# A segment-recurrent attention and a gated feed-forward on one core: softmax products split anew, query pieces in another order, weights loaded in halves, four feed-forward units moved into the loop

## The chip, the cores and the metric

The kernel runs on one core of a Trainium2 chip. Its engines run side by side: TensorE (PE in the profile, with its weight loads as PEld), VectorE (DVE), ScalarE (ACT), GpSimd (POOL) and SyncE (SP), which issues the DMAs. The metric is the device time of one execution in microseconds (us), the median of several.

## The reference

The input x has 2048 rows of 512. The first part, A, normalizes x and walks over it in 64 segments of 32 rows. The eight rows of memory that a segment's attention leaves are the first eight of the next segment's 40 rows, so the segments form a chain:

```
mem = mem0
for s in range(64):
    h = concatenate([mem, xs])            # 8 + 32 rows, 512 wide
    q, k, v = h @ Wq, h @ Wk, h @ Wv      # 32 heads of 128
    scores = q k^T * 128**-0.5            # masked, 40 x 40 for each head
    o = softmax(scores) v @ Wo
    mem = o[:8]; outs.append(o[8:])
```

The second part, B, takes h = x + A, normalizes it, computes z = gelu(h_n @ w_in) (1792 wide), splits z into z1 and z2 of 896 each, normalizes z2 over its columns, mixes it over rows with a 2048 x 2048 matrix w_sp, adds b_sp, multiplies by z1, and multiplies by w_out (896 x 512). The output is h plus that.

## The kernel before, in words

Everything is issued through an emitter: each operation names the tokens that it reads and writes, and the emitter makes the semaphore waits from them. The order of the calls is the order on each engine. Nothing is reordered later, so the order written in the file is what counts.

The kernel has three stages.

The *prologue* loads the weights in the order Wq, Wk, Wv, Wo. `load_w` (L304 to L309) loads a quarter of one of the first three (8 heads, 1 MB) with one DMA and one token. It normalizes the first rows of x, transposes them (`xT`, L383) and computes q and k of the x rows of chunk 0 (16 segments) and half of chunk 1 before the loop starts (`qkx_mm`, L418, called by `start_x`; one call is a group of 16 matmuls: four heads of Wq for i below 8, four of Wk from 8 on).

The *loop* runs over the 64 segments (L1035 on). The rows of x of a segment do not depend on the memory, so products of them alone for later segments are cut into units that fill the places where TensorE would wait for other engines. One list of units, `gx`, gives one whole unit to each segment, just before the products of the probabilities with V. A second list, `gv`, gives single quarters of a unit ("atoms"). `vx_group` units make V rows, `qkx_group` and `qkr_group` make q and k columns. In the last segments units of part B take their place: `z2_group` and `z2_atoms` compute the z2 half of z for 128 rows in narrow tiles (32 columns of the array at a time), 448 wide.

Within a segment, TensorE goes through these steps, and this order is written out by hand:

1. `QK` (L500, L501): q and k of the segment's 40 rows for two halves of the heads, in pieces of four matmuls of 512 columns, one piece for each 128 of the 512 inputs (dc 0 to 3). The pieces of the first two dc need the first half of the new memory, `hT`, which ACT copies (L707), and the others the second. Then `QK_evac`: ACT copies the sums into a staging tile `Tst` (L537), DVE transposes it from there into QT or KT (L549). `mask_put` (L561, DVE) writes the mask into the scores' bank. `K1` and `K1_transpose` (L527, L534) do the fourth product, in two halves.
2. `S_half` (L571, L577): scores of one half of the heads, on top of the mask. `sm_exp` (L585) on ACT, `sm_sums` (L592) on TensorE, `sm_ln` and `sm_rcp` (L603, L607) on ACT give the reciprocal R of the softmax denominators.
3. `V_half` (L500, in between) and `V_evac` (L635 on ACT, L637 on DVE): V of the segment.
4. `sm_norm` (L611): E times R, 160 columns of each half, on POOL for half 0 and on DVE for half 1; `sm_normx` (L617, DVE), the 64 columns against the x keys that the unit above prepared.
5. the unit from `gx` or `zx`, then `PV_half` (L645, L651), the scaling copies `cT_evac` (L664 ACT, L666 DVE), and `Wo`, which ends in `part` and `mem_out` (L702, L707): the next segment's memory.

A small planner (L1004 to L1030) keeps the instruction stream of TensorE in step with a period of 256 instructions: `tile_mm` can use a weight tile that the piece before has loaded (`held`, L501) or load it again (L500). `plan` weighs where the period's boundary falls in the next segments, and where it asks for it `hold` lets up to eight pieces load again, which adds four instructions each. Its constants are WAITS = 15 and 2 per segment.

*Stage B* starts after the loop. `z2_row` and `z2_mm` (L1264) make z2 for rows 13 to 15; rows 0 to 12 come back from DRAM. Then, for each of twelve row blocks in turn, it mixes a block (`mix0`, L1303, five matmuls), computes two groups of z1 (`z1_some`, L1296, four matmuls of 512 columns each, evacuated by ACT at L1299 with the gelu), and brings the z2 of the next block through gelu (L1327), statistics (L1278, L1280, DVE), the power on POOL (L1282, L1284) and the scaling (L1289, DVE). The 28 z1 groups are counted off in pairs; the mixing of the second to fourth quarter of the columns and the output products (L1420) follow.

Of the kernel before, what the change touches and what calls it, by code (L numbers as in the profile page):

```python
# [169 lines left out]
def fast_path(nc, st, keep, A_x, A_mem0, A_Wq, A_Wk, A_Wv, A_Wo, A_seg_len, B_w_in, B_w_sp, B_b_sp, B_w_out, out):  # L170
# [15 lines left out]
    CK = 16  # L186
# [71 lines left out]
    z2p_d = nc.dram_tensor("z2p_d", [NP, 128, FH], BF, kind="Internal").ap()  # L258
    wT_d = nc.dram_tensor("wT_d", [S // 64, 128, RB, 64], BF, kind="Internal").ap()
# [50 lines left out]

    load_xe(0, 0)
    load_xe(1, 1)
    for hq in range(4):
        load_w(0, hq)
# [95 lines left out]
    def qkx_mm(ck, i, bank, only_hh=None, only_dc=None):  # L410
        mi, h0 = i // 8, 4 * (i % 8)
        ws = (w_q, w_k)[mi]
        for hh in range(4):
            h = h0 + hh
            for dc in range(DC):
                if only_hh is not None and (hh, dc) != (only_hh, only_dc):
# [3 lines left out]
                   reads=[("hTe", ck % 3), ("W", mi, h // 8)], writes=[PB(bank)])  # L420
# [162 lines left out]
    def sm_exp(b):  # L583
        bank = SBK[b]
        act(lambda e: e.activation(out=E_sb[:, b, :], in_=ps[:, bank, 0:224], func=ACT.Exp, scale=scale, bias=SHIFT),  # L585
            reads=[PB(bank)], writes=[("E", b), ("Ex", b)])

    def sm_sums(b):
        bank = SBK[b]
        for c in range(4):  # L590
# [3 lines left out]
               reads=[("E", b), "ones"], writes=[PB(bank)])  # L594
# [15 lines left out]
    def sm_norm(b, on):  # L610
        on(lambda e: e.tensor_tensor(out=E_sb[:, b, 0:160], in0=R_sb[:, b, :], in1=E_sb[:, b, 0:160], op=ALU.mult),  # L611
           reads=[("R", b), ("E", b)], writes=[("E", b)])
# [6 lines left out]
    def V_half(s, b, dcs=range(DC), held=None):  # L619
# [3 lines left out]
        for dc in dcs:  # L623
            for c in range(4):
# [3 lines left out]
                   reads=[("hTx", (s // 4) % 3), ("hTm", s, dc // 2), ("W", 2, 2 * b), ("W", 2, 2 * b + 1)], writes=[PB(bank)])  # L628
# [10 lines left out]
    def PV_half(s, b):  # L639
        xb = s % NVX  # L640
        for g in range(4):
            for c in range(4):
# [5 lines left out]
                    reads=[("V", b, g // 2), ("E", b)], writes=[PB(PVB[c])])  # L648
# [162 lines left out]
    def z2_group():  # L811
        rb, hf = zx.pop(0)
        z2_narrow(rb, hf, XB)
        return lambda: z2_out(rb, hf, XB, "dve")

    def z2_atoms():
        rb, hf = zx.pop(0)
        mms = [lambda dc=dc: z2_narrow(rb, hf, VXB, (dc,)) for dc in range(DC)]
        gv.add(VXB, mms, lambda: z2_out(rb, hf, VXB, "act"))

    Z0 = 42

    def pour():
        if s >= Z0 and not gv.atoms and zx and s + 2 < NSEG:
            z2_atoms()
# [26 lines left out]
    act(lambda e: e.preload_act_table_set("natural_log_exp_and_others"))  # L852
    for j in range(2):
        ln_inplace(j)
    late_consts()
    xT(0, 6)
    xe_copy(0, 6)
    for hq in range(4):
        load_w(1, hq)
# [17 lines left out]
    for i in range(16):  # L877
        start_x(0, i)
        if i == 1:
            xT(1, 7)  # L880
            xe_copy(1, 7)
        if i % 2 == 1 and i > 2:
            start_x(1, i // 2 - 1)
        if 7 <= i < 10:
            ln_apply(i - 3)
        if 6 <= i < 9:
            ln_stats(i - 2)
        if i == 10:
            xT(4, 6)
            ring_copy(0, 6)  # L890
        if i == 12:
            xT(5, 7)
            ring_copy(1, 7)
        if i == 14:
# [3 lines left out]
    start_x(1, 7)  # L898
    for hq in range(4):
        load_w(2, hq)  # L900
# [69 lines left out]
    for ck, i0 in ((1, 10), (2, 0), (3, 0)):  # L970
# [3 lines left out]
        if i0:  # L974
            qkx_group(ck, 10)
            qkx_group(ck, 11)
        for mi, b in ((0, 0), (0, 1), (1, 0), (1, 1))[3 if i0 else 0:]:
# [26 lines left out]
    FETCH, FETCH0, WAITS = 256, 191, 15  # L1004
# [9 lines left out]
    def plan(s, start, depth=4):  # L1014
        n = 588 + 24 * (s % 4 == 2) + 8 * (s >= 3 * CK)
        best = None
        for k in range(9):
            c = 10 * block_cost(start, 4 * k, n) + k
            if depth > 1:
                c += plan(s + 1, start + n + 4 * k + 2, depth - 1)[0]  # L1020
# [12 lines left out]
    zx = [(rb, hf) for rb in (0, 4, 1, 5, 2, 6, 3, 7, *range(8, NP)) for hf in range(2)]  # L1033
    qx_copy(0)
    for s in range(NSEG):  # L1035
# [15 lines left out]
        spare[0] = plan(s, pe_count[0] + WAITS + 2 * s)[1] if s else 0  # L1051
# [11 lines left out]
        QK(s, 1, 0, (2, 0, 1, 3), 2, 3, hold(2))  # L1063
# [61 lines left out]
        sm_norm(0, pool)  # L1125
        sm_normx(0)
        V_evac(1, (0,))
        V_evac(1, (1,), "act")
        sm_norm(1, dve)
        sm_normx(1)  # L1130
        if s == 0:
# [3 lines left out]
            start_x(1, 8)  # L1135
# [4 lines left out]
        full = full or s >= 3 * CK  # L1140
        late = [] if full else pour()
        if s >= 3 * CK:
# [1085 lines left out]
```

## Time and profile before

| | |
|---|---|
| median of 3 runs | 845.12 us (843.77 to 845.2) |
| profiled execution | 842.99 us |
| its span, first to last instruction | 841.3 us |
| instructions | 44,814 |
| TensorE busy | 827.7 us, 98% of the span |
| DVE, ACT, POOL busy | 524.0, 469.1, 127.4 us |
| DMA | 77.29 MB, mean 92 GB/s |

The profile's times are microseconds from the first instruction. A row of a timeline gives the start, the length, the engine, the line of the kernel, the operation, what it writes and reads, its shape, how many instructions it stands for, and in brackets the idle time of the engine before it with what ended that. TensorE's ends are modelled, because its matmuls are pipelined: the next row often starts a little before the end of the last. For the length of a step the differences between starts are the better measure.

### The profile page before, as it was taken

How to read it: one execution, taken by the hardware profiler on the slowest of the kernel's cores; microseconds unless marked ns; L12 is line 12 of the kernel's file. 1: busy time of each engine (PE TensorE's matmuls, PEld its weight loads, DVE VectorE, ACT ScalarE, POOL GpSimd, SP SyncE). 2: the span in 40 equal slices, each digit the busy share in tenths (PEclk: the TensorE clock that was granted, in tenths of full speed). 3: DMA queues.
4: the chain of work that ended last, by engine and by line, in shares of the span. 5: the costliest groups of instructions: out<-in, count | busy, mean ns of one | idle time of the engine just before them, and what ended most of it. 6: DMA issues, size and time to landing. Idle time of an engine off the chain costs nothing.

```text
span 841.3 us, 44814 instructions
## 1 busy us (share of the span) xinstructions
PE 827.7 (98%) x21935; PEld 427.5 (51%) x18845; DVE 524.0 (62%) x1320; ACT 469.1 (56%) x1251; POOL 127.4 (15%) x340
## 2 busy tenths in 40 slices
PE   6999999999999999999999999999999999999998
PEld 6754445555555554555555545455555544444443
DVE  3555667666666666676766676666666666554443
ACT  3456566766666666666666666666666676500000
POOL 5111111111111111111211111111111123200000
PEclk9999999999999999999999999999999999999999
DMA  9962222222222232121323232333323298033001
GB/s 319 379 220 55 78 61 64 71 58 68 56 54 49 59 48 66 38 68 48 82 42 88 54 71 54 84 77 87 85 69 81 74 276 286 1 113 109 30 14 40
DMA packets 111252, 77.29 MB, mean 92 GB/s; under 512 B 64840, under 2 KB 100688, under 8 KB 111056
## 3 DMA queue, kind: packets, MB, share of 16 engines
q1 hardware_dynamic: 111056, 74.36, 31.1%
q8 instruction: 162, 2.65, 1.3%
q14 instruction: 34, 0.28, 0.1%
HBM read 42.38 MB, written 21.59 MB: 76 GB/s over the span
## 4 chain that ended last, share of the span: by engine, by line
PE 97%; DMA 1%; SPq 1%; issue 0%; DVE 0%; ACT 0%
PE f_ps L500 45%; PE f_ps L501 13%; PE f_ps L1303 12%; PE f_ps L729 4%; PE f_ps L1296 3%; PE f_ps L1420 3%; PE f_ps L645 3%; PE f_ps L437 2%; PE f_ps L797 2%; PE f_ps L418 2%; PE f_ps L571 1%; DMA f_arena<-in_A_Wk_dram 1%; PE f_ps L592 1%; PE f_ps L443 1%; PE f_ps L702 1%; PE f_ps L651 1%
## 5 line engine op out<-in xcount | busy, mean ns | idle before, releaser
L500 PE MATMUL f_ps<-f_arena,f_hT 128*32 128x512 bf16 (+1 forms) x4832 | 356.2, 356 | 0.3
L500 PEld LDWEIGHTS f_ps<-f_arena,f_hT 128*32 128x32 bf16 x4832 | 119.8, 96 | 155.6 <-issue 63.5
L501 PE MATMUL f_ps<-f_arena,f_hT 128*32 128x512 bf16 (+1 forms) x2336 | 186.7, 334 | 0.0
L537 ACT ACTIVATE f_Tst<-f_ps 128x512 bf16<-128x512 f32 x228 | 129.4, 597 | 60.3 <-PE f_ps L500 60.3
L500 PE MATMUL f_ps<-f_arena,f_cT 128*32 128x256 bf16 x3844 | 129.1, 272 | 0.9 <-ACT f_cT L664 0.5
L500 PEld LDWEIGHTS f_ps<-f_arena,f_cT 128*32 128x32 bf16 x3844 | 94.4, 96 | 29.0 <-ACT f_cT L664 19.1
L1303 PE MATMUL f_ps<-f_arena 128*128 128x512 bf16 x448 | 100.9, 379 | 0.0
L549 DVE STREAM_TRANSPOSE f_QT<-f_Tst 128x256 uint32<-128x256 uint32 x128 | 57.1, 446 | 67.5 <-ACT f_Tst L537 67.5
L637 DVE CAST f_V_sb<-f_ps 128x512 bf16<-128x512 f32 (+1 forms) x128 | 71.0, 555 | 41.9 <-PE f_ps L500 41.9
L666 DVE TENSOR_SCALAR f_cT<-f_ps 128x320 bf16<-128x320 f32 x128 | 56.9, 486 | 27.8 <-PE f_ps L651 27.8
L1303 PEld LDWEIGHTS f_ps<-f_arena 128*128 128x128 bf16 x448 | 43.7, 98 | 52.6
L585 ACT ACTIVATE f_E_sb<-f_ps 128x224 bf16<-128x224 f32 x128 | 46.2, 361 | 36.4 <-PE f_ps L577 36.4
L695 DVE CAST f_part<-f_ps 128x256 bf16<-128x256 f32 x64 | 27.2, 425 | 61.9 <-PE f_ps L500 61.9
L556 POOL COPY f_QT<-f_arena 128x128 uint32<-128x128 uint32 x64 | 18.7, 292 | 298.4 <-PE f_ps L577 298.3
L664 ACT ACTIVATE f_cT<-f_ps 128x320 bf16<-128x320 f32 x128 | 49.0, 435 | 22.6 <-PE f_ps L651 22.6
L707 ACT ACTIVATE f_hT<-f_ps 128x16 bf16<-128x16 f32 x126 | 23.2, 184 | 53.6 <-PE f_ps L702 53.2
L1309 DVE TENSOR_TENSOR f_arena<-f_ps,f_arena 128x512 f32<-128x512 f32 x28 | 19.3, 690 | 52.9 <-PE f_ps L1303 52.9
L561 DVE CAST f_ps<-f_mask 128x224 f32<-128x224 bf16 x128 | 47.0, 367 | 0.0
L607 ACT ACTIVATE f_R_sb<-f_R_sb 128x160 f32<-128x160 f32 x128 | 43.1, 337 | 4.0
L527 ACT ACTIVATE f_Tst<-f_ps 128x256 bf16<-128x256 f32 x128 | 42.1, 381 | 3.7
L686 POOL COPY f_cTx<-f_cT 128x256 bf16<-128x256 bf16 x64 | 25.4, 396 | 121.0 <-DVE f_cT L666 121.0
L693 ACT ACTIVATE f_part<-f_ps 128x256 bf16<-128x256 f32 x64 | 24.6, 384 | 31.4 <-PE f_ps L500 31.4
(123 smaller groups left out, 1202.1 us busy)
## 6 DMA issues: line engine op xcount, KB each, us to landing
wT_d<-f_wst SPq DMA_DIRECT2D x64, 128.0 KB, 2.3
f_arena<-wT_d SPq DMA_DIRECT2D x32, 256.0 KB, 4.9
f_arena<-in_A_Wq_dram SPq DMA_DIRECT2D x4, 1024.0 KB, 8.7
f_arena<-in_A_Wk_dram SPq DMA_DIRECT2D x4, 1024.0 KB, 14.0
f_arena<-in_A_Wv_dram SPq DMA_DIRECT2D x4, 1024.0 KB, 14.6
f_arena<-in_A_Wo_dram SPq DMA_DIRECT2D x8, 512.0 KB, 9.6
f_Vx<-vext_d SPq DMA_DIRECT2D x63, 64.0 KB, 2.7
vext_d<-f_Vs SPq DMA_DIRECT2D x24, 128.0 KB, 2.0
```

What stands on the lines that cost most here:

```text
L500: return e.matmul(out, lhsT=lhsT, rhs=rhs, start=start, stop=stop, skip_group_check=True, tile_position=(0, 32 * c))
L501: return e.add_instruction(mybir.InstMatmult(name=nc.get_next_instruction_name(), ins=[e.lower_ap(rhs), e.lower_ap(lhsT)], outs=[e.lower_a ...
L527: act(lambda e: e.activation(out=Tst[:, 1, 256 * k:256 * k + 256].rearrange("p (gi r) -> p gi r", r=2), in_=ps[:, bank, 0:256].rearrange(" ...
L537: act(lambda e: e.activation(out=Tst[:, tb, :].rearrange("p (C gi r) -> p C gi r", C=2, r=2), in_=ps[:, bank, :].rearrange("p (C r gi) -> ...
L549: dve(lambda e: e.transpose(out=dst, in_=Tst[:, mi, :].bitcast(U32)), reads=[("T", mi, 0), ("T", mi, 1)], writes=wr)
L561: dve(lambda e: e.tensor_copy(out=ps[:, bank, 0:224], in_=mask[:, :]), reads=["mask"], writes=[PB(bank)])
L585: act(lambda e: e.activation(out=E_sb[:, b, :], in_=ps[:, bank, 0:224], func=ACT.Exp, scale=scale, bias=SHIFT), reads=[PB(bank)], writes=[ ...
L607: act(lambda e: e.activation(out=R_sb[:, b, :], in_=R_sb[:, b, :], func=ACT.Exp, scale=-1.0, bias=RBIAS), reads=[("R", b)], writes=[("R", b)])
L637: dve(lambda e: e.tensor_copy(out=V_sb[:, b, cs], in_=ps[:, bank, cs]), reads=[PB(bank)], writes=wr)
L664: act(lambda e: e.activation(out=dst, in_=src, func=ACT.Copy, scale=UNSC), reads=[PB(PVB[c])], writes=[("cT", c)])
L666: dve(lambda e: e.tensor_scalar(out=dst, in0=src, scalar1=UNSC, scalar2=None, op0=ALU.mult), reads=[PB(PVB[c])], writes=[("cT", c)])
L1303: pe(lambda e: e.matmul(ps[:, bank, 0:TB], lhsT=z2[:, sc, fb * 128:(fb + 1) * 128], rhs=wTb[tb % 2][:, :, sc, :], start=(n == 0), stop=(n ...
```

## The change

Six things are changed together.

- *Prologue.* The first quarter of Wq is loaded by two DMAs. Wk and Wv are loaded in halves (2 MB, one DMA for both quarters' tokens). 40 and 12 matmuls on a constant tile are put ahead of the first transposition and after it. The groups of chunk 0 and chunk 1 are interleaved in pairs: all 16 groups of Wq first, then those of Wk; 28 groups stand before the loop instead of 24, and the units that are left for the loop begin at group 14 instead of 10. The four units of `qkr_group` for chunk 1 are no longer needed.
- *Query order.* The dc 0 piece of the product for half 1 of q moves ahead of the pieces that need the first half of the memory.
- *Softmax products.* The E token is split in two parts (columns 0 to 119 and 120 to 159). For half 1 DVE multiplies the first part and POOL the second, V's first half is evacuated ahead of `sm_normx(0)`, and PV's groups wait for the part of E that they read. The wait for Vx is moved to the last piece of `V_half`.
- *Feed-forward units.* Four of the 28 z1 groups are computed in the loop as narrow units of 512 columns, stored to DRAM, loaded again in front of stage B and put through the gelu there (`z1_gelu`). z units start at segment 44 instead of 48.
- *Stage B.* The z2 of row block 13 is computed in narrow tiles. `check_flag`, which guards a slower path that is not taken here, multiplies with its operands exchanged.
- *Planner.* WAITS is 12 instead of 15 and the step 1 per segment instead of 2.

The diff, cut to its core:

```diff
+    def load_wh(mi, hf):
+        wd, ws = ((A_Wq, w_q), (A_Wk, w_k), (A_Wv, w_v))[mi]
+        wr = wd.rearrange("(dc p) h e -> p dc (h e)", p=128)
+        c0, c1 = hf * 16 * DH, (hf + 1) * 16 * DH
+        tok = [("W", mi, 2 * hf), ("W", mi, 2 * hf + 1)]
+        sp(lambda e: e.dma_start(ws[:, :, c0:c1], wr[:, :, c0:c1]), writes=tok)
...
-    for hq in range(4):
+    for h in range(2):
+        sp(lambda e, h=h: e.dma_start(w_q[:, :, 512 * h:512 * h + 512], wq0[:, :, 512 * h:512 * h + 512]), writes=[("W", 0, 0) if h else "W0"])
+    for hq in range(1, 4):
         load_w(0, hq)
...
-    def sm_norm(b, on):
-        on(lambda e: e.tensor_tensor(out=E_sb[:, b, 0:160], in0=R_sb[:, b, :], in1=E_sb[:, b, 0:160], op=ALU.mult),
-           reads=[("R", b), ("E", b)], writes=[("E", b)])
+    def sm_norm(b, on, hs=(0, 1)):
+        q = slice((0, 120)[hs[0]], (120, 160)[hs[-1]])
+        tok = [("E", b, h) for h in hs]
+        on(lambda e: e.tensor_tensor(out=E_sb[:, b, q], in0=R_sb[:, b, q], in1=E_sb[:, b, q], op=ALU.mult),
+           reads=[("R", b), *tok], writes=tok)
...
+    def load_z1w():
+    def z1_narrow(tb, fb, bank, dcs=range(DC)):
+        for dc in dcs:
+            for c in range(4):
+                q = slice(32 * c, 32 * c + 32)
+                pe(lambda e, dc=dc, q=q, c=c: e.matmul(ps[q, bank, :], lhsT=hTe[:, 1 + fb, dc, q], rhs=xts[tb][:, :, dc, :],
+                                                       start=(dc == 0), stop=(dc == DC - 1), tile_position=(0, 32 * c)),
+    def z1_out(tb, fb, bank, eng):
...
-    Z0 = 42
+    Z0, ZG = 42, 44
...
+    spin(40)
     xT(0, 6)
     xe_copy(0, 6)
-    for hq in range(4):
-        load_w(1, hq)
+    spin(12)
+    for hf in range(2):
+        load_wh(1, hf)
...
-    for i in range(16):
-        start_x(0, i)
+    first = [(ck, i) for i0 in range(0, 8, 2) for ck in range(2) for i in (i0, i0 + 1)]
+    first += [(0, i) for i in range(8, 12)] + [(1, i) for i in range(8, 12)] + [(0, i) for i in range(12, 16)]
+    for n, (ck, i) in enumerate(first):
+        start_x(ck, i)
...
-    FETCH, FETCH0, WAITS = 256, 191, 15
+    FETCH, FETCH0, WAITS, STEP = 256, 191, 12, 1
...
+        QK(s, 1, 0, (0,), 0, 3)
         QK(s, 0, 1, (1,), 0, 2)
         QK(s, 0, 0, (1, 2, 3), 0, 3, hold(1))
...
-        QK(s, 1, 0, (2, 0, 1, 3), 2, 3, hold(2))
+        QK(s, 1, 0, (2, 1, 3), 0, 3, hold(2))
...
-            V_half(s, 1, (2,))
+            V_half(s, 1, (2,), also=[("Vx", s % NVX)])
...
         sm_norm(0, pool)
+        V_evac(1, (0,))
         sm_normx(0)
-        V_evac(1, (0,))
         V_evac(1, (1,), "act")
-        sm_norm(1, dve)
+        sm_norm(1, dve, (0,))
+        sm_norm(1, pool, (1,))
         sm_normx(1)
...
-    z1list = [(tb, fb) for tb in range(NTB) for fb in range(FB)]
+    z1list = [(tb, fb) for tb in range(NTB) for fb in range(FB) if (tb, fb) not in Z1]
...
-        z2_mm(rb, 0, zbank())
+        z2_mm(rb, 0, zbank(), True)
         if k == 0:
             F_group(RB - 1, XB)
-        z2_mm(rb, 1, zbank())
+        z2_mm(rb, 1, zbank(), True)
...
     z2_scaled(len(norm))
+    for u in Z1:
+        z1_gelu(*u)
     z1_some(28)
```

More of the change, by code (lines that the diff above doesn't have):

```diff
@@ L852, in fast_path, with spin @@
     act(lambda e: e.preload_act_table_set("natural_log_exp_and_others"))
+    def spin(n):
+        for _ in range(n):
+            pe(lambda e: e.matmul(ps[:, 0, 0:160], lhsT=onesrc[:, 0:128], rhs=onesrc[:, 0:160], start=True, stop=True),
+               reads=["onesrc"], writes=[PB(0)])
     for j in range(2):
@@ L897, in fast_path @@
             mem0_transpose(7)
-    start_x(1, 7)
-    for hq in range(4):
-        load_w(2, hq)
+    for hf in range(2):
+        load_wh(2, hf)
     wor = A_Wo.rearrange("h e d -> e h d")
@@ L1049, in fast_path @@
             load_xe(3, 1)
[L1051 removed]
+        spare[0] = plan(s, pe_count[0] + WAITS + STEP * s)[1] if s else 0
         QK(s, 0, 0, (0,), 0, 3)
```

102 lines of the change are left out of this document (63 added, 39 removed).

## The prediction, made before the result

> **What bounds the kernel now.** I read the page's head and its chain of waits first, then busy time by stretch (columns: length, busy time and instruction count of each engine, granted clock, DMA share, GB/s), then timelines of the places that the diff touches (start, length, instruction, count, idle time before it and its releaser).
>
> ```profile
> span 841.3 us, 44814 instructions
> PE 827.7 (98%) x21935; PEld 427.5 (51%) x18845; DVE 524.0 (62%) x1320; ACT 469.1 (56%) x1251; POOL 127.4 (15%) x340
> PE 97%; DMA 1%; SPq 1%; issue 0%; DVE 0%; ACT 0%
> ```
> ```profile
> 0.00:34.26 34.26, 26.75 (x468) 25.22 (x469) 14.04 (x26) 12.77 (x19) 13.04 (x55) 1.00 0.96 344
> 34.26:684.00 649.74, 647.92 (x20731) 333.05 (x17632) 428.30 (x1144) 424.49 (x1184) 97.99 (x249) 1.00 0.30 76
> 684.00:841.30 157.30, 153.02 (x742) 69.20 (x745) 81.69 (x150) 31.86 (x49) 16.41 (x36) 1.00 0.30 104
> ```
>
> TensorE carries 97% of the chain. Three stages have different limits: a prologue in which the DMA is 0.96 busy at 344 GB/s, the loop of 64 segments with 1.8 us without a matmul in 649.74, and stage B. The clock is 1.00 throughout, so a gain must be matmuls or a wait taken out. The profiled execution took 842.99 us, 1.69 beyond its span and 2.13 under the median of 845.12; I add the sum to 842.99 and then the 2.13.
>
> **Prologue: Wq's first quarter split, warm-up matmuls, Wk and Wv in halves, chunks interleaved.** TensorE first, then a piece of the chain of waits.
>
> ```profile
> 7.86 3.57 PE L418 MATMUL f_ps<-f_hTe,f_arena 128*128 128x128 bf16 x32 [1.49 <-DMA f_arena<-in_A_Wq_dram]
> 11.91 8.84 PE L418 MATMUL f_ps<-f_hTe,f_arena 128*128 128x128 bf16 x144
> 21.02 3.76 PE L418 MATMUL f_ps<-f_hTe,f_arena 128*128 128x128 bf16 x64 [0.27 <-DMA f_arena<-in_A_Wk_dram]
> 30.95 0.41 PE L383 MATMUL f_ps<-f_ident,f_part 128*32 128x128 bf16 x16
> 31.48 2.85 PE L418 MATMUL f_ps<-f_hTe,f_arena 128*128 128x128 bf16 x48
> 34.26 0.40 PE L500 MATMUL f_ps<-f_arena,f_hT 128*32 128x512 bf16 x4
> ```
> ```profile
> 9.40 11.48 DMA f_arena<-in_A_Wk_dram
> ```
> A group is 16 matmuls: three from 31.48 to 34.26 are 0.93 us each. A transposition of x (L383) is 0.41 less a pipelined end, about 0.34. The first two groups are slow (3.57 for 32) and wait 1.49 for Wq. The split lands half a quarter earlier (a quarter is 1 MB, 2.7 us of a queue at about 390 GB/s), and the 52 spin matmuls run while TensorE waits anyway (it is idle until 5.75 and again for the 1.49). What ends the stage is Wk: the first quarter lands at 9.40 + 11.48 = 20.88, and the bytes and their order ahead of it are unchanged. Half of Wk is one transfer and one token, so the first Wk group now waits for two quarters: 20.88 + 2.7 = 23.6, and 0.14 from landing to matmul (20.88 to 21.02) makes 23.74. All 16 Wq groups stand ahead of it now, not 11: 16 x 0.93 = 14.8 from about 7.2 (7.86 less the half quarter, plus the lag of one more issue), plus two transpositions, is 22.7. So TensorE is done 1.0 early and waits. From the Wk wait to the loop it was 34.26 - 21.02 = 13.24 for 13 groups and three transpositions; now it is 12 groups and two: 13.24 - 0.93 - 0.34 = 12.0. The loop starts at 23.74 + 12.0 = 35.74: **+1.5**, for 28 groups done instead of 24. Bounds: +1.2 (the half lands as fast as its bytes at 392 GB/s) and +2.0 (the second half is late too, or a slower transfer).
>
> The Trainium skill, "TensorE: Matmul & The Clock Gate", Part 1, says that the array runs at half rate until about 3.4 us of busy time have passed. The trace agrees: 3.57 for 32 against 2.85 for 48. By that page alone the spin would bring 32 x 0.052 = 1.7 us; here the Wk wait swallows it.
>
> **Loop, Q order.** Segment 31, like the other 62 after the first; TensorE, its weight loads, then ACT and DVE.
>
> ```profile
> 365.27 0.39 PE L501 MATMUL f_ps<-f_arena,f_hT 128*32 128x512 bf16 x4
> 365.48 0.39 PE L500 MATMUL f_ps<-f_arena,f_hT 128*32 128x512 bf16 x4
> 368.53 0.27 PE L571 MATMUL f_ps<-f_QT,f_KT 128*32 128x40 bf16 x16
> ```
> ```profile
> 364.82 0.12 PEld L500 LDWEIGHTS f_ps<-f_arena,f_hT 128*32 128x32 bf16 x8 [0.36 <-ACT f_hT L707]
> ```
> ```profile
> 365.49 1.09 ACT L537 ACTIVATE f_Tst<-f_ps 128x512 bf16<-128x512 f32 x2 [0.72 <-PE f_ps L500]
> 367.44 0.66 ACT L527 ACTIVATE f_Tst<-f_ps 128x256 bf16<-128x256 f32 x2
> ```
> ```profile
> 366.12 0.45 DVE L549 STREAM_TRANSPOSE f_QT<-f_Tst 128x256 uint32<-128x256 uint32 x1 [0.32 <-ACT f_Tst L537]
> 366.49 0.37 DVE L561 CAST f_ps<-f_mask 128x224 f32<-128x224 bf16 x1
> 366.77 0.42 DVE L549 STREAM_TRANSPOSE f_KT<-f_Tst 128x256 uint32<-128x256 uint32 x1
> 367.11 0.37 DVE L561 CAST f_ps<-f_mask 128x224 f32<-128x224 bf16 x1
> 367.42 0.45 DVE L549 STREAM_TRANSPOSE f_QT<-f_Tst 128x256 uint32<-128x256 uint32 x1
> 367.86 0.59 DVE L534 STREAM_TRANSPOSE f_KT<-f_Tst 128x128 uint32<-128x128 uint32 x2
> ```
>
> One piece of four matmuls takes 0.215 (365.27 to 365.48). A piece of QK(1,0) moves ahead of those that wait for ACT's copy of the memory (the PEld row's releaser). That wait costs about 0.027, the gap being a little over the pitch; it goes. But QK(0,0) now ends 0.215 - 0.027 = 0.19 later, and with it the row of DVE work that leads to the scores. That row begins at 366.12; it will at 366.31. Its starts give 0.37, 0.28, 0.34 and about 0.28 for the first four, 0.37 for the second QT, and some 0.55 for the two KT halves (0.59 with a wait for ACT's pair, which ends at 368.10). Back to back: 366.31 + 2.19 = 368.50, and 0.05 from DVE to TensorE makes 368.55. S_half(1) started at 368.53, waiting for nothing. So the stall moves from the memory copy to the scores: +0.02 per segment, 63 x 0.022 = **+1.4**. Bounds: -1.7 (DVE keeps pace, the 0.027 is gained) and +6 (ACT's later copies must now wait for DVE to free the staging tile, and 0.1 of semaphore time is put on a chain without slack).
>
> **Loop, softmax products.** DVE, then POOL, ACT and TensorE of the same segment.
>
> ```profile
> 369.86 0.23 DVE L617 TENSOR_TENSOR f_E_sb<-f_R_sb,f_E_sb 128x64 bf16<-128x64 f32 x1
> 370.00 0.42 DVE L637 CAST f_V_sb<-f_ps 128x256 bf16<-128x256 f32 x1
> 370.43 0.33 DVE L611 TENSOR_TENSOR f_E_sb<-f_R_sb,f_E_sb 128x160 bf16<-128x160 f32 x1
> 370.67 0.22 DVE L617 TENSOR_TENSOR f_E_sb<-f_R_sb,f_E_sb 128x64 bf16<-128x64 f32 x1
> ```
> ```profile
> 369.97 0.49 POOL L611 TENSOR_TENSOR f_E_sb<-f_R_sb,f_E_sb 128x160 bf16<-128x160 f32 x1 [0.75 <-ACT f_R_sb L607]
> ```
> ```profile
> 370.46 0.38 ACT L635 ACTIVATE f_V_sb<-f_ps 128x256 bf16<-128x256 f32 x1
> ```
> ```profile
> 370.81 0.31 PE L645 MATMUL f_ps<-f_E_sb,f_V_sb 32*128 32x40 bf16 x16
> 370.96 0.20 PE L651 MATMUL f_ps<-f_E_sb,f_Vx 32*128 32x64 bf16 x4
> ```
> ```profile
> 540.67 0.51 DVE L611 TENSOR_TENSOR f_E_sb<-f_R_sb,f_E_sb 128x160 bf16<-128x160 f32 x1
> ```
> ```profile
> 540.51 0.49 POOL L611 TENSOR_TENSOR f_E_sb<-f_R_sb,f_E_sb 128x160 bf16<-128x160 f32 x1 [1.03 <-ACT f_R_sb L603]
> ```
>
> The second PV half starts 0.05 behind DVE's product (370.76) and its last four matmuls 0.07 behind the small product (370.89). This holds in 34 segments; in the others (18 with z units, the early ones with Vx units) PV's end is set a little later by other work. V's evacuation goes first now, so ACT's half of it starts and ends about 0.13 earlier. DVE's product shrinks from 160 to 120 columns: (0.33 - 0.22)/96 is 1.1 ns per column, so 0.28 instead of 0.33. If nothing else happened, PV would end 0.05 earlier: 34 x 0.05 = -1.7. But the 40 columns left go to POOL, which is free from 370.46 and starts them at about 370.54, in the middle of DVE's product (370.42 to 370.71 in the new order). The two rows at 540 show what such a meeting costs: DVE started 0.16 after POOL and took 0.51 instead of 0.33, ending 0.18 after POOL's end; POOL kept its 0.49. The order that I take is POOL's part next, about 0.3 long (an estimate: the 160 columns take 0.49, of which part is fixed) and so ending about 370.84, then DVE's small product, which ends at about 370.90 instead of 370.89: +0.017 in 34 segments and +0.008 in the 18 z segments, **+0.7**. Bounds: -1.7 (no meeting) and +4.0 (DVE's small product goes first, POOL ends near 370.96, and the fourth group of the second PV half waits for it: 34 x 0.08 + 18 x 0.07).
>
> The Trainium skill, "SBUF — State Buffer", section "SBUF: two separate sides", has GpSimd and a VectorE operation with two SBUF inputs share one port pair under an exclusive lock, the second blocking for the whole of the first. It speaks against the new split; the rows at 540 agree.
>
> **Loop, the rest.** Four units of 512 columns go (the last products of chunk 1, done in the prologue), four of 512 (z1) come in; as group units they meet segments with 448-wide z2 units: an estimate of 16 x 64 columns at 0.215/4/512 per column is 0.11 each, two of them so: **+0.2** (0 to +0.4). The wait for Vx is moved into V_half, long after Vx lands, and the planner's constants follow the one wait fewer: 0. Its fetch positions may meet stalls or spare them; the loop's 1.8 us without a matmul bounds that at about ±1.8.
>
> **Stage B: four z1 groups fewer, narrow z2.** TensorE, DVE, POOL and ACT where z1 runs out.
>
> ```profile
> 727.43 1.89 PE L1296 MATMUL f_ps<-f_arena 128*128 128x512 bf16 x8
> 729.16 5.13 PE L1303 MATMUL f_ps<-f_arena 128*128 128x512 bf16 x23
> ```
> ```profile
> 728.02 1.15 DVE L1278 BATCH_NORM_STATS2 f_st<-f_arena 128x6 f32<-128x448 bf16 x2 [1.03 <-ACT f_arena L1327]
> 730.56 0.51 DVE L1289 TENSOR_SCALAR f_arena<-f_arena,f_mv,f_rs 128x896 bf16<-128x896 bf16 x1 [0.77 <-POOL f_rs L1284]
> ```
> ```profile
> 727.05 0.94 ACT L1327 ACTIVATE f_arena<-f_arena 128x896 bf16<-128x896 bf16 x1
> ```
>
> Two groups are 727.43 to 729.16 = 1.73; four are 3.46. But they covered the layer norm of the last two rows: gelu, statistics and POOL's root lead to the scaled row at 730.56 + 0.51 = 731.07. Without z1, gelu starts when ACT is free, one every 0.94, and the chain of statistics (1.15 each) runs on DVE alone: the last scaled row comes at about 729.97 and the mixing matmuls wait some 1.09 for the last two. Gain 3.46 - 1.09 = 2.37. Row 13's z2 in narrow tiles saves the change of tile shape beside narrow F and Wo work, about 0.2. The four z1 gelus (under 0.94 each, the length for 896 columns) fall to an idle ACT after the last norm, and the four loads stand on SP behind b_sp, ahead of w_T and w_out, which feed only what comes after the first mix. **-2.55** (-3.7 with no stall, -1.2 with a longer one).
>
> **Sum.** 1.5 + 1.4 + 0.7 + 0.2 - 2.55 = +1.25: 844.2 for a profiled run, **846.4** against the median. The measurement cannot tell less than 0.2% (843.4 to 846.8) from no change.
>
> **Rivals.** *The port takes DVE's small product first* (slower): the price is +4.0 in place of +0.7, 849.7. It decides if POOL's part ends after 370.90 by that segment's clock. For: DVE's two products stand back to back; against: POOL is there first. *ACT's copies wait for the staging tile* (slower): 0.05 to 0.1 per segment more on the scores' chain, +3 to +6, 849.5 to 852; against: by the order DVE has read the tile before ACT is at the next copy. *No meeting on the port*: -1.7 for +0.7, 844.0. *DVE keeps pace with the scores*: -1.7 for +1.4, 843.3; with the port's gain too, or fetch stalls spared (1.8), 841 to 842. *The prologue does not do what it says*: with Wk landing in quarters' time its +1.5 would be 0: 844.9; the token speaks against.
>
> **How the numbers follow.** Forecast 0.32 (own range 844.6 to 848.2; faster 0.03, same 0.18, slower 0.11). No meeting on the port 0.20 (faster 0.13 with fewer fetch stalls, same 0.07). DVE keeps pace 0.20 (faster 0.16, same 0.04). Small product first 0.16, all slower. ACT's copies wait 0.12 (slower 0.11, same 0.01). Together 0.32, 0.30, 0.38. The range 841.5 to 850.5 leaves out the two ends where two such cases add up.
>
> **What the new profile would show.** The loop's first matmul near 35.7 behind a wait of about 1.0 for Wk. No ACT releaser at the third QK piece, and a DVE (L534's line) release at S_half(1), or none if the rival holds. POOL's 40 columns beside DVE's, with one of them lengthened, and the small product behind it. In stage B, matmuls of the mix waiting on DVE's scaling for about 1.1. The forecast fails if a segment's length moves by more than 0.05 (3 us in all), or the loop starts before 35.

## The result, and the profile after

The changed kernel takes 846.33 us (median of 22 runs, 844.71 to 850.36) beside 845.09 for the kernel before in the same comparison (22 runs, 842.47 to 846.54). The ratio is 1.0021 with a 95% interval of 1.0014 to 1.0027 (the quotient of the two medians, 1.0015, lies within it): slower by 1.2 to 2.3 us. The forecast was 846.4. The profiled execution took 846.08, 1.7 beyond its span.

The head of the page, then busy time by stretch (prologue, loop, stage B), as shown for the kernel before:

```profile
span 844.4 us, 45280 instructions
PE 833.4 (99%) x22069; PEld 432.4 (51%) x19109; DVE 517.7 (61%) x1321; ACT 465.7 (55%) x1250; POOL 148.1 (18%) x404
PE 95%; DMA 2%; SPq 1%; ACT 1%; DVE 1%; issue 0%; POOL 0%
```
```profile
0.00:35.87 35.87, 33.00 (x584) 31.47 (x584) 15.37 (x28) 14.28 (x21) 13.12 (x55) 1.00 0.96 356
35.87:687.00 651.13, 648.08 (x20662) 331.60 (x17708) 419.98 (x1142) 417.82 (x1177) 118.11 (x312) 1.00 0.30 75
687.00:844.40 157.40, 152.34 (x829) 69.28 (x817) 82.40 (x152) 33.59 (x53) 16.85 (x37) 1.00 0.32 109
```

Still one engine, but no longer it alone: ACT, DVE and POOL stand in the chain with 1% or less each, and POOL is busy for 148.1 instead of 127.4, which is the 64 added products.

The span grew by 3.1, more than the medians' 1.24, because the profiled run of before was one of its fastest (842.99). I therefore compare segment by segment: from the first score matmul of one to that of the next (scores 0 and scores 1 are the first score matmuls of half 0 and half 1, PV the products of the probabilities with V). Most segments of a kind agree within 0.01; some single ones take 0.05 to 0.8 more than their neighbours, mostly at other places in the two kernels. Over the usual length these add up to about 2.2 us in the profile of before and 3.3 in that of after. The usual lengths, in ns:

| segment | before | after | difference | of it, scores 0 to scores 1 | of it, scores 1 to last PV matmul |
|---|---|---|---|---|---|
| with a Vx unit (1 to 7) | 10061 | 10069 | +8 | +15 | -2 |
| with a q/k unit (most of 12 to 43) | 9946 | 10009 | +63 | +17 | +37 |
| with a z unit (from 44 on) | 9933 | 9980 | +47 | +17 | +29 |

What is left of each difference lies between the last PV matmul and the next segment's scores. A usual length is itself good to some 9 ns: in other kernels with the same segments one with a q/k unit takes 10000 (z1 spread, planner's constants, below). Set against the forecast, by stretch: the loop starts at 35.87 instead of 34.26 (+1.6; forecast +1.5); the usual lengths of the loop, the four wider units among them, add about 3.0 (forecast 2.3); from the scores of segment 63 to the end it is 161.2 instead of 163.7 (-2.5; forecast -2.55). Together about +2.1, within the interval.

TensorE in the prologue, then the chain of waits there:

```profile
8.41 13.63 PE L432 MATMUL f_ps<-f_hTe,f_arena 128*128 128x128 bf16 x240
23.84 2.84 PE L432 MATMUL f_ps<-f_hTe,f_arena 128*128 128x128 bf16 x48 [1.45 <-DMA f_arena<-in_A_Wk_dram]
35.87 0.40 PE L514 MATMUL f_ps<-f_arena,f_hT 128*32 128x512 bf16 x4
```
```profile
9.60 14.10 DMA f_arena<-in_A_Wk_dram
```

The 240 matmuls of Wq run without the slow start, and the wait for half of Wk is there, 1.45 long: the half lands at 9.60 + 14.10 = 23.70, and the matmuls start 0.14 later. Stage B where z1 runs out, TensorE and then DVE:

```profile
728.72 4.75 PE L1356 MATMUL f_ps<-f_arena 128*128 128x512 bf16 x20
733.90 16.34 PE L1356 MATMUL f_ps<-f_arena 128*128 128x512 bf16 x74 [0.43 <-DVE f_arena L1342]
```
```profile
732.07 1.15 DVE L1331 BATCH_NORM_STATS2 f_st<-f_arena 128x6 f32<-128x448 bf16 x2
733.38 0.46 DVE L1342 TENSOR_SCALAR f_arena<-f_arena,f_mv,f_rs 128x896 bf16<-128x896 bf16 x1
```

The scaling ends at 733.84, and the mix goes on at 733.90. From 728.72 to the first output product at 750.08 are 94 matmuls of 0.2155 (20.26) in 21.36: a stall of 1.1, as the forecast had it.

### The profile page after: what moved, and what is told of

Its sections match the earlier page's. It is cut to its first block, busy times and chain, and to the rows that moved or that the text cites. A ratio compares the mean times of both kernels' runs of the same rounds, so it can differ in the third digit from the quotient of the medians.

```text
span 844.4 us, 45280 instructions
## 1 busy us (share of the span) xinstructions
PE 833.4 (99%) x22069; PEld 432.4 (51%) x19109; DVE 517.7 (61%) x1321; ACT 465.7 (55%) x1250; POOL 148.1 (18%) x404
## 4 chain that ended last, share of the span: by engine, by line
PE 95%; DMA 2%; SPq 1%; ACT 1%; DVE 1%; issue 0%; POOL 0%
PE f_ps L514 44%; PE f_ps L515 12%; PE f_ps L1356 11%; PE f_ps L745 4%; PE f_ps L1480 3%; PE f_ps L661 3%; PE f_ps L1349 2%; PE f_ps L813 2%; PE f_ps L451 2%; PE f_ps L432 2%; PE f_ps L585 2%; DMA f_arena<-in_A_Wk_dram 2%; PE f_ps L606 1%; PE f_ps L457 1%; PE f_ps L718 1%; PE f_ps L667 1%
## 5 line engine op out<-in xcount | busy, mean ns | idle before, releaser
L514 PE MATMUL f_ps<-f_arena,f_hT 128*32 128x512 bf16 (+1 forms) x4972 | 358.9, 355 | 0.2
L514 PEld LDWEIGHTS f_ps<-f_arena,f_hT 128*32 128x32 bf16 x4972 | 124.5, 95 | 149.3 <-issue 58.5
L515 PE MATMUL f_ps<-f_arena,f_hT 128*32 128x512 bf16 (+1 forms) x2196 | 175.3, 333 | 0.0
L551 ACT ACTIVATE f_Tst<-f_ps 128x512 bf16<-128x512 f32 x224 | 127.1, 597 | 64.3 <-PE f_ps L514 58.9
L627 POOL TENSOR_TENSOR f_E_sb<-f_R_sb,f_E_sb 128x160 bf16<-128x160 f32 (+1 forms) x128 | 51.5, 402 | 61.7 <-ACT f_R_sb L621 55.4
```

The costliest lines, as they stand in the source:

```text
L514: return e.matmul(out, lhsT=lhsT, rhs=rhs, start=start, stop=stop, skip_group_check=True, tile_position=(0, 32 * c))
L515: return e.add_instruction(mybir.InstMatmult(name=nc.get_next_instruction_name(), ins=[e.lower_ap(rhs), e.lower_ap(lhsT)], outs=[e.lower_a ...
L551: act(lambda e: e.activation(out=Tst[:, tb, :].rearrange("p (C gi r) -> p C gi r", C=2, r=2), in_=ps[:, bank, :].rearrange("p (C r gi) -> ...
L627: on(lambda e: e.tensor_tensor(out=E_sb[:, b, q], in0=R_sb[:, b, q], in1=E_sb[:, b, q], op=ALU.mult), reads=[("R", b), *tok], writes=tok)
```

## Experiments

All start from the changed kernel. Times are compared with the kernel before on the same chip (843.8 to 843.95 there), so the ratios are to be set beside the 1.0021 above. All the intervals given but that of the last run overlap 1.0014 to 1.0027, so the times alone do not tell the parts apart; the lengths in the profiles do, one profile for each kernel. Positions within a segment are in ns from the first score matmul of half 1, as medians over segments with a q/k unit.

**The softmax products undone.**

```diff
-        V_evac(1, (0,))
         sm_normx(0)
+        V_evac(1, (0,))
         V_evac(1, (1,), "act")
-        sm_norm(1, dve, (0,))
-        sm_norm(1, pool, (1,))
+        sm_norm(1, dve)
         sm_normx(1)
```

> The changed kernel with the softmax products as they were before: the first half of V evacuated behind the first small product, and all 160 columns of half 1 on DVE. In the changed kernel's trace the stretch from the scores of half 1 to the last PV matmul is 2477 ns in a segment with a q/k unit (before: 2441), 2479 in one with a z unit (2449), 2579 with a Vx unit (2581). Theory (DVE's small products are blocked while POOL multiplies): these go back to 2441 and 2449, which is 34 x 0.036 + 18 x 0.030 = 1.8 us, so 846.3 - 1.8 = 844.5. Rival (the new wait positions and code places on TensorE made the stretch longer): nothing comes back, 846.3.

Measured: 844.55, ratio 1.0012 (1.0003 to 1.0021). A segment with a q/k unit takes 9967 instead of 10009, one with a z unit 9942 instead of 9980. Scores 1 to the last PV matmul come back to 2454 and 2455, not all the way to 2441 and 2449. What holds them there is another edit of the change, which the list above does not name: one matmul of the second PV half (the last of its second group of four) now waits for V's second part, where only the next one did. With V's evacuation back in its place ACT's copy of that part ends at 2310 and this matmul starts at 2365; in the kernel before it starts at 2325, and the next one waits (2367).

**Only the order of V's evacuation changed** (the split undone).

```diff
-        sm_norm(1, dve, (0,))
-        sm_norm(1, pool, (1,))
+        sm_norm(1, dve)
```

> Only the order of V's evacuation and the first small product stays changed; DVE multiplies all 160 columns of half 1, POOL has one product per segment. Theory (blocking by POOL's operations, of which the first is enough): the first small product still falls into POOL's first product and ends at its end plus 0.08, DVE's large product starts 0.045 later than before and ends 0.33 after that, the second small product ends about 0.045 later: the stretch is about 2480, the time that of the changed kernel, 846.3 within 0.5. Rival (PV waits for POOL's second product): without that the stretch is 2441 and the time 844.5.

**Only the split changed** (the order undone).

```diff
-        V_evac(1, (0,))
         sm_normx(0)
+        V_evac(1, (0,))
```

> Only the split of half 1's product between DVE (120 columns) and POOL (40) stays changed; V's evacuation stands behind the first small product again. Theory: the first small product is back at 0.23 and DVE's 120 columns start where they did before, but POOL's 40 columns start only 0.08 behind its first product and last 0.31, to 0.08 before where the second small product ends, so that this one is still held: stretch about 2477, time 846.3 within 0.5. Rival (the first small product's delay is the cause): stretch 2441 or less, time 844.5 or less.

Measured: 845.03, ratio 1.0014 (1.0002 to 1.0026), and 844.74, ratio 1.0010 (1.0002 to 1.0019). In both the stretch is 2453 or 2454, so neither alone costs what both together do; both numbers of the theory were wrong. A segment with a q/k unit takes 9980 with the order alone and 9972 with the split alone, 13 and 5 more than with both undone (9967), and 42 more with both. The groups of products by shape show why. The columns are count, total busy time, mean ns of one, and idle time before. First the changed kernel:

```profile
L633 DVE TENSOR_TENSOR f_E_sb<-f_R_sb,f_E_sb 128x64 bf16<-128x64 f32 x128 | 38.8, 303 | 0.0
L627 POOL TENSOR_TENSOR f_E_sb<-f_R_sb,f_E_sb 128x40 bf16<-128x40 f32 x64 | 20.0, 313 | 7.4 <-ACT f_R_sb L621 2.1 <-ACT f_V_sb L651 0.4
L627 DVE TENSOR_TENSOR f_E_sb<-f_R_sb,f_E_sb 128x120 bf16<-128x120 f32 x64 | 17.6, 274 | 0.2 <-ACT f_R_sb L621 0.2
```

The same with only the order changed:

```profile
L633 DVE TENSOR_TENSOR f_E_sb<-f_R_sb,f_E_sb 128x64 bf16<-128x64 f32 x128 | 34.6, 270 | 0.0
L627 DVE TENSOR_TENSOR f_E_sb<-f_R_sb,f_E_sb 128x160 bf16<-128x160 f32 x64 | 20.2, 315 | 0.2 <-ACT f_R_sb L621 0.2
```

The same with only the split:

```profile
L633 DVE TENSOR_TENSOR f_E_sb<-f_R_sb,f_E_sb 128x64 bf16<-128x64 f32 x128 | 32.4, 253 | 4.3 <-ACT f_R_sb L621 0.2
L627 POOL TENSOR_TENSOR f_E_sb<-f_R_sb,f_E_sb 128x40 bf16<-128x40 f32 x64 | 18.1, 284 | 7.4 <-ACT f_R_sb L621 2.1 <-POOL f_E_sb L627 0.4
```

And with both undone:

```profile
L633 DVE TENSOR_TENSOR f_E_sb<-f_R_sb,f_E_sb 128x64 bf16<-128x64 f32 x128 | 28.4, 222 | 4.2
```

And DVE, POOL and TensorE in one segment of the changed kernel (its scores of half 1 start at 371.86):

```profile
373.54 0.34 DVE L633 TENSOR_TENSOR f_E_sb<-f_R_sb,f_E_sb 128x64 bf16<-128x64 f32 x1
373.80 0.27 DVE L627 TENSOR_TENSOR f_E_sb<-f_R_sb,f_E_sb 128x120 bf16<-128x120 f32 x1
373.99 0.28 DVE L633 TENSOR_TENSOR f_E_sb<-f_R_sb,f_E_sb 128x64 bf16<-128x64 f32 x1
```
```profile
373.31 0.89 POOL L627 TENSOR_TENSOR f_E_sb<-f_R_sb,f_E_sb 128x160 bf16<-128x160 f32 x2 [0.74 <-ACT f_R_sb L621]
```
```profile
374.13 0.32 PE L661 MATMUL f_ps<-f_E_sb,f_V_sb 32*128 32x40 bf16 x16
374.33 0.21 PE L667 MATMUL f_ps<-f_E_sb,f_Vx 32*128 32x64 bf16 x4
```

The small product takes 222 ns undisturbed and 303 on average in the changed kernel. With the order changed the first small product of a segment (about 333 instead of 225) starts when POOL already multiplies, ends 0.08 behind POOL, and DVE's large product starts 45 ns later. With the split alone POOL's 40 columns take 284, and the second small product is held until they are done (about 280 instead of 218); it ends at 2375, and the first of the PV matmuls that need it starts at 2435, 2 later than with both undone. This is hardly felt, because the wait for V, at 2365 again, holds the matmuls ahead of it. With both, the later large product holds POOL's 40 columns up (313), and these the second small product: it ends at 2408, and the last of the PV matmuls that need it starts at 2477. So the meetings on the two engines are a chain of three, and together they cost more than each alone. The order alone does reach TensorE, though: its second small product ends at 2386, the last four PV matmuls are released by it, together, from 2443 on, and the rest of the segment follows some 12 ns later (6418 from the last of them to the next scores, 6406 without). Why that rest is longer is not shown.

The Trainium skill, "SBUF — State Buffer", section "SBUF: two separate sides", has the port shared between VectorE's operations with two SBUF inputs and GpSimd as a lock that the first comer holds for its whole operation. For the small products the trace agrees: when POOL was first, they end about 0.08 after its product, whenever they started. For POOL's 40 columns it agrees too: they start while DVE's large product still runs, for 0.16 with the split alone and 0.20 with both, and end 0.12 after it either way (2297 after 2176, 2330 after 2210). So 284 is no undisturbed length; the shortest, 260 in segment 25, is where no product of DVE runs beyond the first 0.05 of POOL's.

**The query order undone.**

```diff
-        QK(s, 1, 0, (0,), 0, 3)
         QK(s, 0, 1, (1,), 0, 2)
...
-        QK(s, 1, 0, (2, 1, 3), 0, 3, hold(2))
+        QK(s, 1, 0, (2, 0, 1, 3), 2, 3, hold(2))
```

> The changed kernel with the query pieces in the order of before. Theory (the chain through ACT and DVE to the scores got a late start that is worth more than the wait for the memory copy that went): scores of half 0 to those of half 1 go back from 1109 to 1093 ns, the wait of 0.03 for ACT's copy of the memory returns; 63 x 0.016 = 1.0 us less, 845.3. Rival (the order gains the wait and costs nothing else): 63 x 0.027 = 1.7 us more, 848.0.

Measured: 845.12, ratio 1.0011 (1.0002 to 1.0021), and segments of 10000 instead of 10009 (q/k), 9972 instead of 9980 (z), 10060 instead of 10069 (Vx). Score matmuls of two segments, first with the order undone, then in the changed kernel:

```profile
361.19 0.27 PE L585 MATMUL f_ps<-f_QT,f_KT 128*32 128x40 bf16 x16
362.29 0.27 PE L585 MATMUL f_ps<-f_QT,f_KT 128*32 128x40 bf16 x16
```
```profile
370.75 0.28 PE L585 MATMUL f_ps<-f_QT,f_KT 128*32 128x40 bf16 x16
371.86 0.27 PE L585 MATMUL f_ps<-f_QT,f_KT 128*32 128x40 bf16 x16
```

From half 0 to half 1 it is 1.10 against 1.11 (1092 and 1109 exactly), so the chain over DVE does run late: its last transposition of K ends 1042 behind the scores of half 0, and 1010 with the order undone. But 8 of the 17 ns come back ahead of half 0. The wait for the memory copy that goes is worth 28 there (the starts of the two pieces behind the copy are 233 and 226 apart with the order undone, 215 in the changed kernel), and the scores of half 0 lose 20 of them, since DVE's transposition of K for that half now ends 55 ahead of them instead of 249. By this pair the order costs 9 ns net, 63 x 9 = 0.6 us, which is no more than the usual lengths differ between kernels with the same segments. Theory and rival were each half of it.

**The prologue: Wk in quarters; no warm-up; both.**

```diff
-    for hf in range(2):
-        load_wh(1, hf)
+    for hq in range(4):
+        load_w(1, hq)
```

> The changed kernel with Wk loaded in quarters, as before the change; everything else stays. Theory (the loop's late start is the wait for a 2 MB transfer): the first quarter of Wk lands near 21 and TensorE, done with the 16 Wq groups and the transposition at 22.3, does not wait; 12 groups and two transpositions follow, and the loop starts at 22.3 + 12.0 = 34.3 instead of 35.87: 1.5 less, 846.3 - 1.5 = 844.8. Rival (the DMA's total sets the start: the weights are not there earlier in smaller pieces): the wait moves to a later group and the loop starts near 35.9, 846.3.

```diff
-    spin(40)
...
-    spin(12)
```

> The changed kernel without the 52 warm-up matmuls. Theory (the wait for Wk swallows what they gain): the first 32 matmuls of the products take 3.57 instead of 2.1, TensorE is done with Wq at about 23.8 in place of 22.3, just when Wk lands, and the loop starts at 35.9 as it did, within 0.2. Rival (what they gain counts): the loop starts 1.5 later, near 37.4.

> Wk in quarters and no warm-up matmuls. Theory: with Wk there at 21 nothing swallows the slow first matmuls, so the loop starts 1.5 later than with quarters and warm-up, 34.3 + 1.5 = 35.8. Rival (the first matmuls wait for Wq's data either way, so the warm-up is worth nothing): 34.3.

Measured: 845.48 with quarters, ratio 1.0018 (1.0007 to 1.0028). The other two were run once each, 845.36 without warm-up and 847.10 with both edits, so for them only the profile counts. The loop starts at 36.23 with quarters, at 35.66 without warm-up and at 36.29 with both. TensorE with quarters, then a piece of its chain:

```profile
8.79 6.43 PE L432 MATMUL f_ps<-f_hTe,f_arena 128*128 128x128 bf16 x112 [0.28 <-DMA f_arena<-in_A_Wq_dram]
15.80 7.31 PE L432 MATMUL f_ps<-f_hTe,f_arena 128*128 128x128 bf16 x128 [0.58 <-DMA f_arena<-in_A_Wq_dram]
25.24 1.96 PE L432 MATMUL f_ps<-f_hTe,f_arena 128*128 128x128 bf16 x32 [0.79 <-DVE f_arena L443]
36.23 0.40 PE L514 MATMUL f_ps<-f_arena,f_hT 128*32 128x512 bf16 x4
```
```profile
5.58 13.59 DMA f_part<-in_A_x_dram
```

No wait for Wk is left, and the loop does not start earlier. Two waits for Wq (0.28, 0.58) and one for DVE (0.79) stand in its place; DVE is late since a tile of x, issued at 5.58, takes 13.59 to land. Without warm-up (first matmuls, then the loop):

```profile
7.16 1.89 PE L432 MATMUL f_ps<-f_hTe,f_arena 128*128 128x128 bf16 x16 [0.71 <-ACT f_hTe L413]
9.52 13.81 PE L432 MATMUL f_ps<-f_hTe,f_arena 128*128 128x128 bf16 x240
35.66 0.40 PE L514 MATMUL f_ps<-f_arena,f_hT 128*32 128x512 bf16 x4
```

The first group takes 1.89 instead of 1.06, the 240 matmuls start 1.1 later, and no wait for Wk follows. So what the warm-up gains is swallowed, as expected, and the transfer's size is not what sets the loop's start. The nine kernels here whose prologue is the changed one start their loops between 35.54 and 36.57, so differences under 1.0 mean nothing; all wait for Wk, 0.5 to 1.5. What sets the start is not settled by these runs. TensorE alone needs 28 groups of 0.93 and the transpositions, 27.6 from about 7, which is 34.6 without any wait, and 1 to 2 us of waits or slow matmuls come on top, at changing places. The DMA is busy throughout, at 350 to 410 GB/s in stretches of 4 us from 6 on, so the total of the weights and x is the likely source; no run here changes that total.

**z1 spread over the last iterations.**

```diff
-        z1_some(2)
+        z1_some(2 if k < 8 else 1)
```

> The changed kernel with the 24 z1 groups of stage B spread otherwise: two per iteration for the first eight of the twelve iterations and one for the last four, where the changed kernel has two in ten and none in the last two. Theory (without z1 the norm of z2 is late, and the mix waits 1.1): an iteration with one group has 1.08 + 0.86 = 1.95 of TensorE work against 1.8 of DVE per row, so the waits fall to 0.3 or less: stage B 0.8 to 1.1 shorter, 846.3 - 0.9 = 845.4. Rival (the wait is set by something in front of these iterations, such as DRAM rows that come late): the wait stays at 1.1, 846.3.

Measured: 844.60, ratio 1.0010 (0.9999 to 1.0022). TensorE there:

```profile
728.90 1.24 PE L1356 MATMUL f_ps<-f_arena 128*128 128x512 bf16 x5
729.98 1.03 PE L1349 MATMUL f_ps<-f_arena 128*128 128x512 bf16 x4
730.84 18.29 PE L1356 MATMUL f_ps<-f_arena 128*128 128x512 bf16 x84
```

84 matmuls in one run without a wait. From 720.27, the start of the same mix, to the output products it is 28.70 (748.97), against 29.78 in the changed kernel (720.30 to 750.08): 1.1 less, the whole stall.

**z1 back in stage B.**

```diff
-    Z1 = [(0, 0), (0, 1), (1, 0), (1, 1)]
+    Z1 = []
...
-    Z0, ZG = 42, 44
+    Z0, ZG = 42, 48
...
-    zx[-2:-2] = [(1, *u) for u in Z1]
```

> The changed kernel with the four z1 groups in stage B again (28 groups, two per iteration in all twelve) and none in the loop; the z2 units start at segment 48 as before, so segments 44 to 47 have no unit. Theory (a segment's length is set by the softmax chain, so a unit in it costs next to nothing): segments 44 to 47 are as long as the others within 0.05, the loop is 0.3 shorter by the wider units, the mix does not wait and stage B is 2.3 longer: 846.3 + 2.0 = 848.3. Rival (a unit costs its TensorE time of 0.86 in the loop as well): the loop is 4 x 0.8 = 3.2 shorter, stage B 2.3 longer, 845.4.

Measured: 847.49 (5 runs), ratio 1.0045 (1.0025 to 1.0064). Segment 44, which has no unit here, and then the same segment of the changed kernel with a z unit (score matmuls at its start and at the next one's):

```profile
491.87 0.28 PE L585 MATMUL f_ps<-f_QT,f_KT 128*32 128x40 bf16 x16
501.81 0.28 PE L585 MATMUL f_ps<-f_QT,f_KT 128*32 128x40 bf16 x16
```
```profile
492.11 0.28 PE L585 MATMUL f_ps<-f_QT,f_KT 128*32 128x40 bf16 x16
502.08 0.28 PE L585 MATMUL f_ps<-f_QT,f_KT 128*32 128x40 bf16 x16
```

TensorE in front of PV in the first of them:

```profile
494.96 0.27 PE L661 MATMUL f_ps<-f_E_sb,f_V_sb 32*128 32x40 bf16 x16 [0.51 <-POOL f_E_sb L627]
```

9.94 without, 9.97 with: the segment has 20 matmuls of 448 columns more (16 of the unit, 4 of the other list), 0.94 us by the 0.215 for four of 512, and they cost 0.03. Without them PV waits 0.51 for POOL's product of half 0, so the softmax chain is what PV starts on. The move of z1 is the part of the change that pays. Stage B was 3.3 longer here, of which 1.0 is a single stall without a releaser at row 13's z2.

**The planner's constants as before.**

```diff
-    FETCH, FETCH0, WAITS, STEP = 256, 191, 12, 1
+    FETCH, FETCH0, WAITS, STEP = 256, 191, 15, 2
```

> The changed kernel with the planner's constants of before (15 and 2 for each segment). Theory (the constants only follow the one wait fewer; the odd long segments come from the code's place in the 256-instruction period and differ in place, not in sum): the sum of what single segments take over their neighbours stays within 1.5 of the changed kernel's 3.7, 846.3 within 0.8. Rival (the constants take stalls away): the sum is 2 or more higher and the time 848 to 849.

Measured: 846.35 (7 runs), ratio 1.0031 (1.0019 to 1.0043), which overlaps with the 1.0021 (1.0014 to 1.0027) of the new constants. Single long segments add up to 3.9, against 3.7 by the same count (which includes the four wide units) with the new constants. No effect of the constants is shown, in either direction.

**The parts that pay, without those that cost.** Softmax products, query order and the wait of the second PV half for V as before; z1 spread as above; everything else as changed.

```diff
-                    reads=[("V", b, g // 2), ("E", b, g // 3), *([("V", b, 1)] if (g, c) == (1, 3) else [])], writes=[PB(PVB[c])])
+                    reads=[("V", b, g // 2), ("E", b, g // 3)], writes=[PB(PVB[c])])
```

> The changed kernel with the softmax products, the query order and the wait of the second PV half for V as before, and z1 in stage B spread two per iteration for eight iterations and one for four. Theory (the two edits in the loop cost 42 and 9 ns per segment, the earlier wait for V 12 more; the late norm 1.1 in stage B): a segment with a q/k unit takes 9946 instead of 10009, one with a z unit 9933 instead of 9980, 34 x 0.063 + 18 x 0.047 = 3.0, and 1.1 in stage B: 846.3 - 4.1 = 842.2, 0.34% under the kernel before. Rival (the parts don't add up, since one wait takes the next one's place): segments of 9.97 or more, 844 to 845, no faster than before.

Measured: 842.06 (11 runs), ratio 0.9983 (0.9973 to 0.9992): faster than both kernels, 1.9 us under the 843.95 of before on that chip. Its page's head, its loop, and two of its segments:

```profile
span 839.6 us, 45152 instructions
```
```profile
35.59:684.00 648.41, 646.33 (x20690) 333.33 (x17736) 428.05 (x1143) 422.19 (x1179) 98.10 (x249) 1.00 0.29 75
```
```profile
369.25 0.27 PE L585 MATMUL f_ps<-f_QT,f_KT 128*32 128x40 bf16 x16
379.19 0.27 PE L585 MATMUL f_ps<-f_QT,f_KT 128*32 128x40 bf16 x16
```

Segments are 9946 and 9933 again, those of before to the ns, so the parts add up: 42 (products) + 9 (query order) leaves 12 of the 63, and the one edit left in this stretch is the second PV half's wait for V's second part, put one matmul earlier. The positions show it: with the products undone the last PV matmul starts at 2453, here at 2441, one matmul of that half less behind the arrival of V. But this wait costs only where V comes late. In the changed kernel ACT's copy ends at 2184, long before the matmul that waits for it, which starts at 2316 right behind its neighbour; there all of the stretch's 37 ns come from the products. So against the kernel before the products cost 54 of the 63 (10000 with the query order undone, 9946 before) and 39 in a segment with a z unit (9972, 9933); undoing them alone gives back 12 less of the 54, because the wait for V then takes their place. The edit of that wait was not run alone.

## Why the prediction was right, step by step

The time was right to 0.1 us, which is luck: of the steps, some were right and others made up for each other.

- **What bounds the kernel**: held in part. Pricing the segments by their waits was right: the chain between engines inside a segment sets its length. But TensorE's 97% was read as if a gain could be matmuls there too; 0.94 us of them put into a segment cost 0.03, and without them TensorE waits.
- **Prologue, +1.5**: measured +1.6, with the wait for Wk where it was forecast (1.45, forecast 1.0). The cause given, half of Wk as one transfer, was wrong: with quarters the loop starts no earlier. So the size is partly luck, the more as starts behind the same prologue spread over 1.0. The rival that gave 844.9 for quarters' time falls as well. What the warm-up brings is swallowed, as stated, but it is 1.1 by the start of the 240 matmuls, not 1.7; without warm-up the loop starts at 35.66.
- **Query order, +1.4**: right in mechanism, too large. The scores of half 1 do wait for DVE's late row, and the stretch between the scores grew by 0.017; but 0.008 come back ahead of the scores of half 0, so the net is 0.009 where 0.022 was forecast, 0.6 at most.
- **Softmax products, +0.7**: the step that was mis-sized. POOL's part does come ahead of the small product, as I chose, but it takes 0.313 and starts behind a large product that is itself late. I had put the end of the second small product 0.01 later; it is 0.05 later. What I left out is the first meeting: V's evacuation ahead of the first small product moves that one into POOL's first product. 34 x 0.054 + 18 x 0.039 = 2.5, between forecast and the bound of 4.0. The rival with the small product first did not occur.
- **Wait for V put earlier**: costed at nothing because I did not speak of it, and in the changed kernel it costs nothing; it holds PV up by 0.012 in a segment once the products are undone.
- **Wider units, +0.2**: segments 59 and 60 took 10.10, 0.12 over their neighbours, and with 58 and 61 it is 0.27.
- **Stage B, -2.55**: -2.5, with the stall of 1.1. The 0.2 for row 13's narrow z2 was not measured alone.
- **Planner, 0**: no effect seen.

The query order was put 0.8 too high and the products 1.8 too low. The sum by stretches is about +2.1 (the loop's terms one by one add up to some 0.4 more than its 3.0, which is what 9 ns in each of some 50 segments make), and the forecast of +1.25 lies at the lower end of the measured 1.2 to 2.3. The predicted 846.4 hit the median partly since the 2.13 between the profiled run and the median was added whole, and part of it is single long segments, which differ from run to run.

## What to carry to other kernels

A unit of work put in where TensorE would wait anyway is nearly free, so moving work there pays by what it leaves behind, and what it leaves behind must then be checked for the cover that it gave (here 1.1 us of layer norm, won back by spreading the rest). An operation moved on one engine changes which operations of two engines meet: follow a blocked operation through all that it delays, since two edits that cost 13 and 5 ns alone can cost 42 together. When an edit is undone, look at which wait takes its place before you read its price from the difference. When a wait is the last one before a stage starts, look at what else arrives at that time before you blame it: taking it away may only show the next.

## What the runs showed of the hardware that was not expected

- DVE's product of 64 columns with two SBUF inputs takes 222 ns alone and ends about 80 ns after POOL's product when it meets one that started first, up to 335 ns in all. POOL's product of 40 columns ends 120 ns after DVE's when DVE was first.
- POOL's product of 40 columns takes 260 ns where it is least disturbed (segment 25) and that of 160 takes 490, so a quarter of the columns costs more than half the time.
- Loops that follow the same prologue start up to 1.0 us apart (35.54 to 36.57), all with a wait for Wk and some with waits for Wq as well.
- Single segments take up to 0.9 us longer than their neighbours, once 1.4 (segment 50 with z1 spread), with no releaser that explains it; together 2 to 4 us of each profile. Some places recur (segment 39 is some 0.25 longer in most of the changed kernels), others differ from kernel to kernel. Their cause stays open, and they are what limits the comparison of kernels this close.
